# First loads in one queue, more tile pairs turned by DMA, one copy on another engine, and the last gate gradient later

## The chip, the cores and the metric

The kernel runs on one core of a Trainium2 chip. The core has a matrix engine (TensorE, called PE in the profile), a vector engine (DVE), a scalar engine (ACT), a general engine (GpSimd, called POOL) and a sync engine (SP) that mainly issues DMA transfers. Sixteen DMA engines move the data. The engines run their own instruction streams, each in order, and wait for one another through semaphores.

The metric is the device time of one execution, in microseconds (us). The median of three runs of the kernel before is 925.81 us (924.9 to 925.99).

## The reference

The program computes a forward pass and seven gradients. S is 2048 tokens, D is 512, F is 1376; there are 32 heads of 16 and an attention window of 256 tokens. In short:

```
g   = sigmoid((x * gate_w).sum(-1))            # one gate for each token
a   = sliding_window_attention(x @ wqkv) @ wo  # 32 heads, window 256
b   = (relu(x @ W_gate) * (x @ W_up)) @ W_down
out = g * a + (1 - g) * b
gradients of out for x, wqkv, wo, W_gate, W_up, W_down, gate_w, given grad_out
```

Both branches are called with x, which is the input `A_x`.

## The kernel before

The kernel has three stages that follow one another on TensorE.

**Stage 1 (up to about 250 us): the feed-forward branch, forward and backward.** The tokens are cut into four groups of 512 (`tg`, `NTG` = 4) and the 1376 hidden columns into eleven chunks of 128 (`fc`, `FC` = 11). That makes 44 steps. A step n does the gate product (`gate`, line 345), the up product (`up`, line 350), and, some steps later, the hidden gradient (`dh`, at step n + 2), the turning of the results by DMA (`turn_h`, `turn_dgu`) and the weight gradients (`weights`, at step n + 6). In the first four steps the loop at line 428 also turns x (`turn_x`), computes the gates of the tokens (`gate_col`), scales grad_out (`db_rows`) and turns that (`turn_db`).

The schedule of a stage is written by hand (`tc.manual_schedule()`): each engine's instructions stand in the order in which the Python code issues them.

Ahead of the first step come the loads. SP's queue issues x of the first group in two halves (line 234), then x of the second group, grad_out of the first, a piece of W_down, and so on (lines 254 to 263), all in the order of the code. ACT's queue issues `gate_w` and the first 128 columns of W_gate and of W_up (lines 237 to 239). Meanwhile TensorE runs eight warm-up products on zeros (`WARM`, lines 206 and 244). Then it turns `gate_w` into a column (`turn_gw`, line 417, called at 425), turns x of the first group (`turn_x(0)`), and starts the first gate product.

**Stage 2 (about 252 to 722 us): attention, forward and backward.** The 32 heads form four groups of eight (`c`), the queries sixteen blocks of 128 (`j`), and each block of queries meets up to three blocks of keys (`kb`). Heads go in two halves of four (`half`). One unit is one (c, j, kb, half); there are 360. Its role is `d` for the block on the diagonal, `m` for the middle one and `f` for the far one. For a unit TensorE makes the scores (`front`, line 656, tile `ST`), ACT takes the exponential (668), GpSimd masks roles d and f (670, 673), TensorE makes the gradient's score product (`front_dp`, 682, tile `dPT`), DVE multiplies (`gradp`, 687), and three units later (`LAG`) TensorE sums rows (`rowsum`, 696 and 698, tile `BA`).

The probabilities and their gradients are also needed turned, as the stationary operand of the products in `cd_piece` (lines 518 and 521, tile `CD`). `flip` (line 707) turns them in one of two ways. With `u.dma` a DMA transpose does it (line 715), for both halves at once where `u.pair` holds, and for one half otherwise. Without `u.dma`, TensorE makes eight transposes (line 725), and ACT and DVE in turn copy the result out of PSUM. The choice is made at lines 643 and 644: role d always goes as a pair; role m as a pair in odd rows of the first three head groups; in the other rows of role m only half 0 goes by DMA; role f never. Pairs of role m live in tile `PPm` (two buffers), single halves in `PPs` (one buffer).

The projections of the next four blocks (`project_parts`, line 118) and the weight gradient of the previous head group (`grad_parts`, line 598) are fed in between units, whenever a running `credit` (line 915) is high enough; a unit with TensorE transposes lowers that credit by 0.44. The projection of Q is scaled and copied out of PSUM by DVE (line 140) into `zT`, is spread by SP into the tile that the score products read (line 499), and is turned by DMA (line 171).

**Stage 3 (about 730 to 925 us): the outputs.** Sixteen tiles of 128 tokens (`t`, line 994). A tile makes the two branches' outputs (lines 1001 and 1005), the gradient of x (tile `dxps`: 22 products at line 1032, then 12 at line 1047), and the gate gradient: DVE and GpSimd compute `dz` from the outputs, `add_dgw` (line 1035) multiplies x with it, one tile late, through `pending_dgw`. Only the last tile has no later tile, so it adds its own share at once (lines 1042 to 1044), and in the middle of its last twelve products the gradient is turned into a row and stored (lines 1050 to 1055). The last instruction of the program is the store of the last `dx_sb` (line 1059).

Of the kernel before, what the change touches and what calls it, by code (L numbers as in the profile page):

```python
# [22 lines left out]
def kernel(  # L23
# [20 lines left out]
    nc = tc.nc  # L44
# [67 lines left out]
    if True:  # L112
        HH = HG // 2
        proj = {}
        groups = [(c, tg) for c in range(DC) for tg in range(NTG)]
        PENG = ("dvs", "dvs")

        def project_parts(c, tg):
            t4 = {}
            proj[(c, tg)] = t4  # L120
            pj = pjA if (c * NTG + tg) % 3 == 0 else pjs["b"]

            def mm(nm, which, eng):
                ps, tag, bufs, _, _ = pools["now"]
                pp = ps.tile([P, TGW], F32, tag=tag, bufs=bufs, name="pp")
                for cd in range(DC):
                    if which < 3:
                        nc.tensor.matmul(pp[:], lhsT=w_p[c][:, cd, which * P:(which + 1) * P], rhs=x_T[tg][:, cd, :],  # L128
                                         start=(cd == 0), stop=(cd == DC - 1))
                    else:  # L130
                        nc.tensor.matmul(pp[:], lhsT=w_p[c][:, cd, 3 * P:4 * P], rhs=da_T[tg][:, cd, :],
                                         start=(cd == 0), stop=(cd == DC - 1))
                if nm in ("Q", "dO"):
                    if nm == "Q":
                        t4["z"] = pjA.tile([P, 2, TGW], BF, tag="zT", name="zT")
                    dst = t4["z"][:, ("Q", "dO").index(nm), :]
                else:
                    dst = pjA.tile([P, TGW], BF, tag="T", bufs=2, name=f"{nm}T")[:]
                if nm == "Q":
                    nc.vector.tensor_scalar(dst, pp[:], scale, None, op0=ALU.mult)  # L140
                else:
                    evac(dst, pp[:], eng)
                t4[nm] = dst
                if nm in ("Q", "dO"):
                    if c == 0 and tg == 0:
                        w = ("Q", "dO").index(nm)
                        for k in range(NP):
                            rows = slice(32 * k, 32 * k + 32)
                            evac(zt[0][rows, w, k, :, :], dst[rows, :].rearrange("p (k q) -> p k q", k=TPG),
                                 (("dve", "act")[w] if k % 2 else "dve"))  # L150
                else:
                    for k in range(2):
                        t4[f"{nm}{k}"] = pj.tile([P, TGW], BF, tag=f"{nm}{k}", name=f"{nm}{k}")
                        if PENG[k] == "act":
                            nc.scalar.mul(t4[f"{nm}{k}"][:], pp[:], par[:, k:k + 1])
                        elif PENG[k] == "dve":
                            nc.vector.tensor_scalar(t4[f"{nm}{k}"][:], pp[:], par[:, k:k + 1], None, op0=ALU.mult)
                        else:
                            nc.vector.tensor_scalar(t4[f"{nm}{k}"][:], dst[:], par[:, k:k + 1], None, op0=ALU.mult)

            def tr(a_nm, b_nm):
                _, _, _, ps, trt = pools["now"]
                pt = ps.tile([P, 2, TPG, P], BF, tag=trt, bufs=2, name="ptp")
                for a, nm in enumerate((a_nm, b_nm)):
                    for k in range(TPG):
                        nc.tensor.transpose(pt[:, a, k, :], t4[nm][:, k * P:(k + 1) * P], ident[:])
                return pt

            def tr_rows():
                rows = pjA.tile([P, 2, TPG, P], BF, tag="rows", bufs=2, name="rows")  # L170
                nc.sync.dma_start_transpose(out=rows[:].rearrange("p a t d -> p (a t) d"),
                                            in_=t4["z"][:].rearrange("p a s -> p (a s)"))
                t4["rows"] = rows

            def tr_kv():
                kv = pj.tile([P, TPG, HG, 34], BF, tag="KV1", name="KV1")
                nc.gpsimd.memset(kv[:, :, :, 0:1], -1.0)
                nc.gpsimd.memset(kv[:, :, :, Dh + 1:Dh + 2], 1.0)
                pt = tr("K", "V")
                v = lambda a: pt[:, a, :, :].rearrange("p k (h d) -> p k h d", h=HG)  # L180
                nc.vector.tensor_scalar(kv[:, :, :, 1:1 + Dh], v(0), scale, None, op0=ALU.mult)
                nc.vector.tensor_copy(kv[:, :, :, Dh + 2:2 * Dh + 2], v(1))
                t4["kv"] = kv

            return [lambda: mm("Q", 0, "dve"), lambda: mm("dO", 3, "dve"), tr_rows, lambda: mm("K", 1, "act"),
                    lambda: mm("V", 2, "act"), tr_kv]

    with ExitStack() as p1, tc.manual_schedule():
# [14 lines left out]
            return ap[tg * TGW:(tg + 1) * TGW, :].rearrange("(t p) d -> p t d", p=P)  # L203

        W0 = P
        WARM = 8
        Wg_v, Wu_v = (w.rearrange("(c p) f -> p c f", p=P) for w in (B_W_gate, B_W_up))
        go_in, da_in = {}, {}

# [23 lines left out]
        for i in range(2):  # L233
            nc.sync.dma_start(x_r[:, i * half:(i + 1) * half, :], rows_of(x_d, 0)[:, i * half:(i + 1) * half, :])
        gw_r = fp.tile([P, P], BF, tag="upm", name="gw_r")
        nc.vector.memset(gw_r[:], 0.0)
        nc.scalar.dma_start(gw_r[0:DC, :], gate_w.rearrange("(c p) -> c p", p=P))
        nc.scalar.dma_start(Wg_sb[:, :, 0:W0], Wg_v[:, :, 0:W0])
        nc.scalar.dma_start(Wu_sb[:, :, 0:W0], Wu_v[:, :, 0:W0])
        nc.vector.memset(tiny[:], 0.0)  # L240
        nc.scalar.activation(tiny[:], tiny[:], ACT.Sigmoid)
        make_identity(nc, ident[:])
        wps0 = ps1.tile([P, TGW], F32, tag="mm", bufs=3, name="warm_ps")
# [6 lines left out]
        def load_wgu(a, b):  # L250
            nc.sync.dma_start(Wg_sb[:, :, a:b], Wg_v[:, :, a:b])
            nc.sync.dma_start(Wu_sb[:, :, a:b], Wu_v[:, :, a:b])

        load_x(1)
        load_go(0)
        nc.sync.dma_start(wd0[:], B_W_down[0:P, :])
        load_x(2)
# [164 lines left out]
        DA0 = 2 * NTG  # L422
        pools["now"] = (ps1, "tr", 2, ps1, "tr")
        first = []
        turn_gw()
        turn_x(0)
        stores = {}
        for n in range(N1 + 8):
            at = lambda lag: steps[n - lag] if 0 <= n - lag < N1 else None
            if at(0):  # L430
                gate(at(0))
                if n < NTG:
                    gate_col(n)
                if n == 2:
                    turn_wd0()
                if n + 1 < NTG:
                    turn_x(n + 1)
                up(at(0))
                if n < NTG:
                    db_rows(n)  # L440
                if at(0).tg == 0 and at(0).fc > 0:
                    turn_wd(at(0).fc)
# [43 lines left out]
    if True:  # L486
# [145 lines left out]
        for c in range(DC):  # L632
            for j in range(NT):
                kbs = [k for k in (j - 1, j, j - 2) if k >= 0]
                for half in range(2):
                    order = kbs if half or len(kbs) < 3 else [kbs[0], kbs[2], kbs[1]]
                    for ki, kb in enumerate(order):
                        u = Unit()
                        u.c, u.j, u.kb, u.half = c, j, kb, half
                        u.first = ki == 0 and half == 0  # L640
                        u.last = ki == len(kbs) - 1 and half == 1
                        u.role = ("d", "m", "f")[j - kb]
                        u.pair = u.role == "d" or (u.role == "m" and j % 2 == 1 and c < DC - 1)
                        u.dma = u.pair or (u.role == "m" and half == 0 and (c < DC - 1 or j < 10))
                        units.append(u)
        NU = len(units)
# [318 lines left out]
    with ExitStack() as p56:  # L965
        x_r5 = x_r

        with ExitStack() as p6:
# [20 lines left out]
            for g in range(NG):  # L989
# [3 lines left out]
                for tl in range(GT):  # L993
# [45 lines left out]

                    if pending_dgw is not None:  # L1040
                        add_dgw(*pending_dgw)
                    if t == NT - 1:
                        add_dgw(t, dz_bf)
                        nc.scalar.copy(dgw_sb[:, 0:DC], dgw_ps[:])
                    pending_dgw = (t, dz_bf)
                    for cc in range(C3):
                        nc.tensor.matmul(dxps[:], lhsT=T_g[:, 4 * (cc % DC) + cc // DC, lsl], rhs=W6[("wqkv", cc)],  # L1047
                                         start=(i == 0), stop=(i == nmm - 1))
                        i += 1
                        if t == NT - 1 and cc == C3 // 2:  # L1050
                            row_ps = ps6r.tile([P, P], BF, tag="aps", bufs=1, name="row_ps")
                            nc.tensor.transpose(row_ps[:], dgw_sb[:], ident[:])
                            row_sb = t6.tile([P, P], BF, tag="row_sb", bufs=1, name="row_sb")
                            nc.scalar.copy(row_sb[0:DC, :], row_ps[0:DC, :])
                            nc.sync.dma_start(out_7.rearrange("(c p) -> c p", p=P), row_sb[0:DC, :])
# [34 lines left out]
```

## Time and profile before

| | |
|---|---|
| median of three runs | 925.81 us (924.9 to 925.99) |
| the profiled execution: time | 926.6 us |
| the profiled execution: span, first to last instruction | 924.9 us |
| busy: TensorE / weight loads / DVE / ACT / GpSimd | 910.0 / 577.1 / 489.9 / 447.2 / 486.4 us |
| mean granted TensorE clock | 0.996 |
| data moved by DMA | 166.49 MB, mean 180 GB/s |

The profile page cuts the span into forty slices of 23 us. These three of its rows give tenths of the slice in which TensorE was busy, tenths of the full clock that TensorE was granted, and tenths that the DMA engines were busy:

```profile
PE   7999999999999999999999999999999999999998
...
PEclk8999999999999999999999999999999999999999
DMA  9889889999699999978999889999999799777841
```

Only the first and last slices show a TensorE that is not fully occupied, and only the first a lower clock. The DMA engines are busy through nearly all of the program. A busy TensorE is not a TensorE at its peak, since products are pipelined and each line counts from its start to its modelled end.

The costliest waits of the other engines are not repeated here: an engine that waits for TensorE, while TensorE is busy, costs nothing by that.

### The profile page before, as it was taken

How to read it: one execution, taken by the hardware profiler on the slowest of the kernel's cores; microseconds unless marked ns; L12 is line 12 of the kernel's file. 1: busy time of each engine (PE TensorE's matmuls, PEld its weight loads, DVE VectorE, ACT ScalarE, POOL GpSimd, SP SyncE). 2: the span in 40 equal slices, each digit the busy share in tenths (PEclk: the TensorE clock that was granted, in tenths of full speed). 3: DMA queues.
4: the chain of work that ended last, by engine and by line, in shares of the span. 5: the costliest groups of instructions: out<-in, count | busy, mean ns of one | idle time of the engine just before them, and what ended most of it. 6: DMA issues, size and time to landing. Idle time of an engine off the chain costs nothing.

```text
span 924.9 us, 26637 instructions
## 1 busy us (share of the span) xinstructions
PE 910.0 (98%) x10878; PEld 577.1 (62%) x10878; DVE 489.9 (53%) x910; ACT 447.2 (48%) x784; POOL 486.4 (53%) x937
## 2 busy tenths in 40 slices
PE   7999999999999999999999999999999999999998
PEld 5566565656657767667776677767777644444443
DVE  3433334435377777657776577766677222222223
ACT  4522322222268777667776677766688301111111
POOL 2644444545276767766777567776677311111111
PEclk8999999999999999999999999999999999999999
DMA  9889889999699999978999889999999799777841
GB/s 300 178 177 197 191 191 200 218 222 204 164 163 164 167 173 170 185 150 163 178 147 183 168 153 172 179 179 180 169 159 206 178 255 238 186 186 185 182 91 47
DMA packets 484635, 166.49 MB, mean 180 GB/s; under 512 B 408800, under 2 KB 483392, under 8 KB 484512
## 3 DMA queue, kind: packets, MB, share of 16 engines
q1 hardware_dynamic: 462808, 142.63, 82.9%
q10 hardware_dynamic: 20072, 17.57, 7.2%
q0 software_dynamic: 1632, 4.59, 1.4%
q8 instruction: 85, 1.39, 0.6%
q14 instruction: 38, 0.31, 0.1%
HBM read 32.28 MB, written 36.24 MB: 74 GB/s over the span
## 4 chain that ended last, share of the span: by engine, by line
PE 81%; POOL 5%; DMA 4%; ACT 3%; issue 3%; DVE 2%; SPq 1%; ACTq 0%; POOLq 0%; DVEq 0%
PE dxps L1032 8%; PE ST L656 7%; PE wps L391 7%; PE dPT L682 7%; PE pt L725 6%; PE dxps L1047 5%; PE wps L611 4%; PE gps L342 4%; PE bps L1001 4%; PE ups L342 4%; PE CD L518 4%; PE dhps L342 3%; PE dps L393 3%; PE BA L696 3%; PE pp L128 3%
## 5 line engine op out<-in xcount | busy, mean ns | idle before, releaser
L670 POOL TENSOR_SCALAR_AFFINE_SELECT PPd<-PPd 128x512 bf16<-128x512 bf16 x128 | 81.2, 634 | 113.8 <-ACT PPd L668 113.0
L687 DVE TENSOR_TENSOR Pd<-Pu,dPT 128x512 bf16<-128x512 bf16 x154 | 103.9, 678 | 67.8 <-POOL Pu L673 63.1
L656 PE MATMUL ST<-z,K 128*128 128x512 bf16 x360 | 135.9, 378 | 3.1 <-ACT PPd L668 0.9
L682 PE MATMUL dPT<-z,V 128*128 128x512 bf16 x360 | 136.0, 378 | 0.7 <-DVE Pd L687 0.2
L668 ACT ACTIVATE Pu<-ST 128x512 bf16<-128x512 f32 x154 | 92.6, 601 | 45.9 <-PE ST L656 45.2
L356 POOL TENSOR_TENSOR hT<-rg,upm 128x512 bf16<-128x512 bf16 x44 | 51.3, 1167 | 117.7 <-DVE upm L354 109.2
L391 PE MATMUL wps<-dgu_r,x_r 128*128 128x256 bf16 (+1 forms) x704 | 103.9, 270 | 0.2
L687 DVE TENSOR_TENSOR PPd<-PPd,dPT 128x512 bf16<-128x512 bf16 x128 | 87.2, 681 | 21.3 <-POOL PPd L670 20.0
L668 ACT ACTIVATE PPd<-ST 128x512 bf16<-128x512 f32 x128 | 77.3, 604 | 22.4 <-PE ST L656 20.2
L391 PEld LDWEIGHTS <-x_r 128*128 128x128 bf16 x704 | 68.3, 98 | 31.0 <-issue 0.7
L673 POOL TENSOR_SCALAR_AFFINE_SELECT Pu<-Pu 128x512 bf16<-128x512 bf16 x112 | 71.7, 640 | 21.2 <-ACT Pu L668 20.4
L1010 ACT COPY a_sb<-aps 128x512 f32<-128x512 f32 x16 | 9.4, 586 | 151.7 <-issue 137.7
L354 DVE SCALAR_TENSOR_TENSOR upm<-rg,ups 128x512 bf16<-128x512 bf16 x44 | 30.1, 684 | 81.4 <-PE ups L342 41.1
L348 ACT ACTIVATE rg<-gps 128x512 bf16<-128x512 f32 x44 | 26.3, 598 | 95.1 <-PE gps L342 54.2
L393 PE MATMUL dps<-db_r,h_r 128*128 128x512 bf16 x176 | 66.7, 379 | 0.0
L366 POOL TENSOR_TENSOR dgu<-dh_sb,rg 128x512 bf16<-128x512 bf16 x44 | 57.5, 1307 | 5.3 <-ACT dh_sb L362 5.3
L725 PE MATMUL pt<-ident,Pd 128*128 128x128 bf16 x616 | 59.5, 219 | 0.0
L725 PE MATMUL pt<-ident,Pu 128*128 128x128 bf16 x616 | 59.0, 217 | 0.0
L1016 POOL DMA_DIRECT2D out_dram<-o_sb x16 | 8.7, 541 | 88.5 <-DVE o_sb L1014 82.1
L72 ACT COPY p<-pt 128x1024 bf16<-128x1024 bf16 x51 | 52.4, 1028 | 1.2
L696 PE MATMUL BA<-KV,Pu 128*128 128x33 bf16 x616 | 51.0, 178 | 0.0
L611 PE MATMUL wps<-rows_st,x_r 128*128 128x384 bf16 x256 | 50.3, 325 | 0.0
(186 smaller groups left out, 2365.2 us busy)
## 6 DMA issues: line engine op xcount, KB each, us to landing
dqkvo_d<-rows_st SPq DMA_DIRECT2D x15, 512.0 KB, 4.0
hT_d<-hT ACTq DMA_DIRECT2D x44, 128.0 KB, 2.6
dgT_d<-dgu ACTq DMA_DIRECT2D x44, 128.0 KB, 2.9
duT_d<-dgu ACTq DMA_DIRECT2D x44, 128.0 KB, 3.0
duT_g<-duT_d SPq DMA_DIRECT2D x8, 640.0 KB, 5.7
gt<-hT_d SPq DMA_DIRECT2D x7, 640.0 KB, 5.5
dgT_g<-dgT_d SPq DMA_DIRECT2D x7, 640.0 KB, 5.7
z<-zT SPq DMA_DIRECT2D x60, 64.0 KB, 2.3
```

The lines of the kernel that those rows point to most:

```text
L342: nc.tensor.matmul(out[:], lhsT=w(c), rhs=x(c), start=(c == 0), stop=(c == DC - 1))
L391: nc.tensor.matmul(acc["w"][:, c, 0:2 * nw], lhsT=x_r[:, t, c * P:(c + 1) * P], rhs=k.dgu_r[:, :, i, s0:P], start=(go_ and c % 2 == 0), st ...
L393: nc.tensor.matmul(acc["d"][:], lhsT=k.h_r[:, i, :], rhs=db_r[:, t, :], start=go_, stop=no_)
L611: nc.tensor.matmul(wps[:], lhsT=x_r[:, t, part * P:(part + 1) * P], rhs=sts[c][:, t, 0:3, :], start=first and t == t0, stop=last and t == ...
L656: nc.tensor.matmul(ST[:], lhsT=KTt[:, ksl], rhs=z[:, 0, :, jl, :], start=True, stop=True)
L668: nc.scalar.activation(u.Pu[:], ST[:], ACT.Exp)
L670: nc.gpsimd.affine_select(out=u.Pu[:], in_=u.Pu[:], compare_op=ALU.is_ge, fill=0.0, base=0, pattern=[[0, HH], [1, P]], channel_multiplier=-1)
L682: nc.tensor.matmul(u.dPT[:], lhsT=VTt[:, ksl], rhs=z[:, 1, :, jl, :], start=True, stop=True)
L687: nc.vector.tensor_tensor(out=u.Pd[:], in0=u.Pu[:], in1=u.dPT[:], op=ALU.mult)
L696: nc.tensor.matmul(BA[:, h, 0:33], lhsT=u.Pu[:, hh, :], rhs=kv[:, u.kb % TPG, h, 1:34], start=(u.first and hh == 0), stop=True, skip_group ...
L725: nc.tensor.transpose(pt[:, a, hh, :], src[:, hh, :], ident[:])
L1032: nc.tensor.matmul(dxps[:], lhsT=src[:, fc, lsl], rhs=W6[(wt, fc)], start=(i == 0), stop=(i == nmm - 1))
```

## The change

- The three loads on ACT's queue move to SP's queue. The first columns of W_gate stand behind the two halves of x; `gate_w` and the first columns of W_up stand behind x of the second group.
- `turn_gw` moves from ahead of the first `turn_x` to behind the first gate product, and in step 0 `gate_col` moves behind the up product. One of eight warm-up products is left out.
- In `project_parts`, Q of the second group (`groups[1]`) is scaled by ACT instead of DVE.
- In head groups 1 and 2, role m of rows 4, 6 and 8 goes as pairs: half 1 is turned by DMA together with half 0, where TensorE turned it.
- In the last tile, the last `add_dgw` and its copy come after four of the last twelve products, and the row is turned after nine instead of seven.

```diff
-                if nm == "Q":
+                if nm == "Q" and (c, tg) == groups[1]:
+                    nc.scalar.mul(dst, pp[:], scale)
+                elif nm == "Q":
                     nc.vector.tensor_scalar(dst, pp[:], scale, None, op0=ALU.mult)
...
-        WARM = 8
+        WARM = 7
...
         gw_r = fp.tile([P, P], BF, tag="upm", name="gw_r")
+        nc.vector.memset(tiny[:], 0.0)
         nc.vector.memset(gw_r[:], 0.0)
-        nc.scalar.dma_start(gw_r[0:DC, :], gate_w.rearrange("(c p) -> c p", p=P))
-        nc.scalar.dma_start(Wg_sb[:, :, 0:W0], Wg_v[:, :, 0:W0])
-        nc.scalar.dma_start(Wu_sb[:, :, 0:W0], Wu_v[:, :, 0:W0])
-        nc.vector.memset(tiny[:], 0.0)
         nc.scalar.activation(tiny[:], tiny[:], ACT.Sigmoid)
...
+        nc.sync.dma_start(Wg_sb[:, :, 0:W0], Wg_v[:, :, 0:W0])
         load_x(1)
+        nc.sync.dma_start(gw_r[0:DC, :], gate_w.rearrange("(c p) -> c p", p=P))
+        nc.sync.dma_start(Wu_sb[:, :, 0:W0], Wu_v[:, :, 0:W0])
         load_go(0)
...
-        turn_gw()
         turn_x(0)
...
                 gate(at(0))
-                if n < NTG:
+                if n == 0:
+                    turn_gw()
+                elif n < NTG:
                     gate_col(n)
...
                 up(at(0))
+                if n == 0:
+                    gate_col(n)
...
-                        u.pair = u.role == "d" or (u.role == "m" and j % 2 == 1 and c < DC - 1)
+                        u.pair = u.role == "d" or (u.role == "m" and c < DC - 1 and (j % 2 == 1 or (c > 0 and j in (4, 6, 8))))
                         u.dma = u.pair or (u.role == "m" and half == 0 and (c < DC - 1 or j < 10))
...
-                    if t == NT - 1:
-                        add_dgw(t, dz_bf)
-                        nc.scalar.copy(dgw_sb[:, 0:DC], dgw_ps[:])
                     pending_dgw = (t, dz_bf)
                     for cc in range(C3):
...
-                        if t == NT - 1 and cc == C3 // 2:
+                        if t == NT - 1 and cc == C3 // 4:
+                            add_dgw(t, dz_bf)
+                            nc.scalar.copy(dgw_sb[:, 0:DC], dgw_ps[:])
+                        if t == NT - 1 and cc == C3 * 2 // 3:
                             row_ps = ps6r.tile([P, P], BF, tag="aps", bufs=1, name="row_ps")
```

## The prediction

> **What bounds the kernel now.** I read the busy shares first: TensorE is busy for 910.0 of 924.9 us, and no other engine passes 53%. Then I asked which waits TensorE has. They are few, and these are the two that the change touches (us in total, times, longest):
>
> ```profile
> PE gps L342 <- DMA Wg_sb<-in_B_W_gate_dram: 3.1, 1, 3.1
> ...
> PE dgw_ps L1037 <- DVE dz_bf L1026: 0.4, 1, 0.4
> ```
>
> So time can only come from TensorE's own work, from its first 15 us, or from its clock. The timeline of the start (start, us, engine, line, operation):
>
> ```profile
> 1.27 3.43 PE L245 MATMUL warm_ps<-warm 128*128 128x512 bf16 x8 [1.27 <-DVE warm L231]
> ...
> 4.59 1.06 PE L276 MATMUL ptx<-ident,x_r 128*128 128x128 bf16 x16
> ...
> 5.70 1.07 ACT L72 COPY x<-ptx 128x512 bf16<-128x512 bf16 x2 [1.22 <-DVE x L74]
> ...
> 8.71 1.89 PE L342 MATMUL gps<-x,Wg_sb 128*128 128x512 bf16 x4 [3.06 <-DMA Wg_sb<-in_B_W_gate_dram]
> ...
> 10.87 1.87 PE L276 MATMUL ptx<-ident,x_r 128*128 128x128 bf16 x16
> ...
> 12.53 1.91 PE L342 MATMUL ups<-x,Wu_sb 128*128 128x512 bf16 x4
> ...
> 14.23 1.24 PE L342 MATMUL gps<-x,Wg_sb 128*128 128x512 bf16 x4
> ```
>
> The operands of the first gate product were ready at 6.77, when ACT's copies end. Its weights came at 8.7. And the same sixteen transposes that took 1.06 us at 4.59 take 1.87 us at 10.87. The stretches say why (PE busy, PEld, DVE, ACT, POOL, granted clock, DMA share, GB/s):
>
> ```profile
> 5.70:8.70 3.00, 0.00 (x0) 0.00 (x0) 0.41 (x1) 1.07 (x2) 0.00 (x0) 0.85 1.08 313
> 8.70:11.00 2.30, 2.29 (x22) 1.20 (x23) 0.00 (x0) 0.36 (x1) 0.00 (x0) 0.50 1.09 353
> 11.00:14.60 3.60, 3.60 (x22) 2.28 (x20) 0.98 (x3) 2.13 (x5) 0.00 (x0) 0.50 1.10 350
> ```
>
> During the idle 3 us the granted clock falls, and it stays at half until 14.6. The wait thus costs itself and half speed on what follows. Why the weights are late, from the transfers (KB, us from issue to landing):
>
> ```profile
> x_r<-in_A_x_dram SPq DMA_DIRECT2D x3, 512.0 KB, 8.1
> ...
> p2m<-PPm SPq DMA_TRANSPOSE x30, 5.2
> ...
> p2m<-PPs SPq DMA_TRANSPOSE x24, 3.7
> ...
> Wg_sb<-in_B_W_gate_dram ACTq DMA_DIRECT2D x1, 128.0 KB, 6.8
> ```
>
> 128 KB take 6.8 us on ACT's queue beside SP's 512 KB loads; the two 256 KB halves of x, ahead of everything in SP's queue, take 3.0 us.
>
> **The start.** Queue order becomes x (512 KB), Wg (128), x1 (512), gate_w (1), Wu (128), go0 (512). At the 313 to 353 GB/s of the rows above 128 KB are 0.4 us; twice that for their short rows gives 0.8. The second x half was issued at 1.28 and landed 3.1 us later, at 4.4; Wg behind it lands near 5.2, x1 1.5 us later near 6.7, gate_w with it, Wu near 7.5, go0 near 9. SP issues three more transfers ahead of go0, at 0.43 to 0.58 us each by ACT's rows: 1.6 us, hidden, since these lines stand behind 1 MB of traffic anyway.
>
> One warm-up matmul less (0.43 us) and the gate_w transpose gone from the front let the x transposes start near 4.3, so the copies end near 6.4. The gate product's first two matmuls can run before that, the last two after: issued by 6.85. Then, at the full-speed spacing of the rows after 16 us: gate_w transpose 0.1, sixteen transposes 0.89, up product 0.86, gate column 0.54. The second gate product starts near 9.3 instead of 14.23: 4.9 us. I take off 0.5 for gate_w or x1 landing a little after 6.85, and use 4.4. If the clock halves all the same, at 7.82 as in this trace, some 3.1 us of that are lost again (6.8 us at half speed, of which the sixteen small gate-column matmuls do not slow): 1.5 is the lower end, 4.9 the upper.
>
> What is late next: x2 (needed near 10.9, lands near 10.9 by the same spacing), then nothing that I can see. The large weight remainders still drain near 24 us, and the turned hidden tiles queue behind them; the first weight-gradient product needs those at 36.8 now, near 32 then. From 24 us to 225 TensorE has no idle row worth 0.1 us, so a microsecond won at the start is a microsecond at the end.
>
> A sentence apart: the Trainium skill ("DMA: Bandwidth & Descriptors", Issuing engines are not separate DMA queues) says that issuing from several engines only saves sequencer time, since all share the same sixteen DMA engines. Read as "the queue does not matter", it would set this part at zero and the whole at 922.8; the 6.8 us against 3.0 agree that the engines are shared, and show that sharing is what delays the first weights.
>
> **Six pairs by DMA.** Units with role m in rows 4, 6, 8 of head groups 1 and 2 now go as pairs. Half 0 went by DMA already; half 1 had eight TensorE transposes and one copy. 48 transposes leave TensorE. One flip in the timeline:
>
> ```profile
> 400.77 0.38 PE L725 MATMUL pt<-ident,Pu 128*128 128x128 bf16 x4
> ...
> 400.99 0.39 PE L725 MATMUL pt<-ident,Pd 128*128 128x128 bf16 x4
> ...
> 401.22 0.38 PE L682 MATMUL dPT<-z,V 128*128 128x512 bf16 x1
> ```
>
> 0.45 us from the first transpose to the next product; 6 x 0.45 = 2.7. TensorE's idle share in 400 to 600 us is 0.74 of 200, so nearly all is real: 2.6 (0 to 2.9). Six copies of 0.68 (DVE) or 1.03 us (ACT) go too; both engines are busy for some 70%, so worth nothing. The DMA side pays 5.2 - 3.7 = 1.5 us for each pair. What hides it is the lead of the products that read the pair: they run when the next row is through, six units of some 1.3 us (360 units between 251.9 and 718.5 us) and the lag of three: 11 us or more after the issue, against a landing of 5.2 (6.7 at most). The longer SP instruction (2.37 us against 1.41, by the rows of the flip line) holds back the spreads of the next Q by 1.0; the first of them is issued at 257.6 and read by the fifth row, eighteen units or 23 us into the stage. The strips where it lands have room (same columns as above):
>
> ```profile
> 410.00:420.00 10.00, 10.00 (x179) 7.61 (x178) 6.78 (x12) 6.74 (x13) 5.91 (x15) 1.00 0.56 129
> ...
> 530.00:540.00 10.00, 10.00 (x193) 7.70 (x192) 6.34 (x13) 7.46 (x13) 6.68 (x17) 1.00 0.55 128
> ```
>
> The planner also gets 0.44 more credit for each of the six, so projections are fed a unit or so earlier: the same work, no price.
>
> **Q of the second group on ScalarE.** It ran on DVE from 253.35 to 254.04, and a score product waited 0.32 us for it. On ACT it takes 0.60 us from 253.35 on, in front of the second exponential, which then ends near 254.55 instead of 254.17; its mask on GpSimd and its gradient product follow 0.4 later. The score product goes 0.1 earlier. Bounds -0.3 to +0.4; I use 0, since ACT has 1.05 us idle before its next exponential but one.
>
> **The last gate gradient.**
>
> ```profile
> 918.38 0.24 PE L1037 MATMUL dgw_ps<-dz_bf,x_r 128*128 128x1 bf16 x4 [0.39 <-DVE dz_bf L1026]
> 918.38 0.14 PEld L1037 LDWEIGHTS <-x_r 128*128 128x128 bf16 x3 [0.46 <-issue]
> ...
> 922.10 0.35 SPq L1059 DMA_DIRECT2D out_dram<-dx_sb  x1
> ```
>
> Four products of 0.22 us now stand ahead of it, so the 0.39 us are filled: 0.4 (0.3 to 0.5). The row's transpose goes two products later, but its store is issued some 1.1 us before the dx store in SP's queue still: nothing.
>
> **Sum.** 4.4 + 2.6 + 0 + 0.4 = 7.4. The profiled execution had a span of 924.9 and a time of 926.6, which becomes 917.5 and 919.2. It lay 0.8 over the median of the runs, 925.81; that becomes 918.4.
>
> **Rivals.**
> Half clock (0.20). The clock falls at the start in spite of the shorter gap. For it: TensorE still pauses near 5.5 to 6.2 for the copies, and a fixed grid of time could catch that; two stretches at 0.50 followed work that was 74% busy. Against: the fall in this trace needed 3 us with no matmul at all. Start 1.5, whole 4.5: 921.3. The Trainium skill ("TensorE: Matmul & The Clock Gate", Part 1: The HAM clock gate) describes a free-running window of about 3.4 us that must be busy to release the clock and idle to lower it, so it would differ from run to run; the 3 us gap here agrees with it.
> The flips are not worth their time (0.07): TensorE fills the gap with other waits, as at 700 or 260 us. Sum 4.8: 921.0.
> One queue gains nothing (0.06): Wg's short rows go slowly and x1 and go0, issued 1.6 us later, are waited for instead. Start 0, whole 3.0: 922.8.
> Slower (0.08): the pairs fill the DMA queue in rows 3 to 9, where every row would now carry two full pairs. Added work 6 x 1.5 = 9.0 us; once the backlog has eaten the 6 us between landing and first use, TensorE waits for the added time instead of saving its transposes: 9.0 against 4.4 + 0.4, so 930.0. It decides from the point where more than 4.8 of the 9.0 stand on the path; short of it the time is near today's. Against it: the DMA share is 0.55 to 0.56 in two of the strips, and no wait of TensorE for a turned pair shows. For it: shares of 1.14 and 1.25 in 400 to 410 and 500 to 510.
>
> **Chances.** The forecast holds with 0.59. The first three rivals are faster too: 0.92. The last splits into slower, 0.05, and same, 0.03 (0.2%, 1.9 us, is about what a measurement of this kernel can tell). Range: from the best of each part, 4.9 + 2.9 + 0.3 + 0.5 = 8.6, to 917.2 and rounded down to 917.0, up to 922.0, which takes in the half clock and the lost flips and leaves out the last two rivals.
>
> **What would show it.** Right: no wait of the first gate product for Wg, a granted clock at 1.0 before 14 us, the second gate product near 9.5 to 10, p2m turned from PPm 36 times and from PPs 18 times (30 and 24 now), 48 fewer transposes at the flip line with no more idle time of TensorE than now in 370 to 560 us, and no 0.39 before the last gate-gradient product. Wrong: 0.50 in the clock after 7 us; waits for p2m or z in rows 4 to 9; a new wait for x or Wu in the first 15 us.

## The result and the profile after

The changed kernel takes 929.15 us (median of 6 runs, 928.31 to 929.77) where the kernel before takes 925.36 (6 runs, 923.14 to 926.2): ratio 1.0044, 95% interval 1.0031 to 1.0057. The forecast was 918.4. The profiled execution took 928.77, with a span of 927.1.

The waits of TensorE in the changed kernel (us in total, times, longest; in the views below, the line of before stands first). The wait for Wg went from 3.1 to 0.7 and the one for dz_bf is gone. But the score products' wait for the exponentials that write PPs, which stood at 0.6 (one time) before, is now the longest, and a wait of the same kind for PPm is new:

```profile
PE ST L656 <- ACT PPs L668: 0.6, 1, 0.6
```
```profile
PE ST L661 <- ACT PPs L673: 6.5, 3, 3.5
PE ST L661 <- ACT PPm L673: 1.3, 1, 1.3
...
PE gps L344 <- DMA Wg_sb<-in_B_W_gate_dram: 0.7, 1, 0.7
...
PE ptg L421 <- DMA gw_r<-in_gate_w_dram: 0.6, 1, 0.6
```

The start answers to the timeline shown of before. The second gate product begins at 10.19 instead of 14.23, and the sixteen transposes at 8.02 take 1.07 where they took 1.87:

```profile
1.27 3.17 PE L244 MATMUL warm_ps<-warm 128*128 128x512 bf16 x7 [1.27 <-DVE tiny L238]
4.23 1.27 PE L278 MATMUL ptx<-ident,x_r 128*128 128x128 bf16 x16
6.16 1.11 PE L344 MATMUL gps<-x,Wg_sb 128*128 128x512 bf16 x4 [0.66 <-DMA Wg_sb<-in_B_W_gate_dram]
7.83 0.23 PE L421 MATMUL ptg<-ident,gw_r 128*128 128x128 bf16 x1 [0.57 <-DMA gw_r<-in_gate_w_dram]
8.02 1.07 PE L278 MATMUL ptx<-ident,x_r 128*128 128x128 bf16 x16
...
10.19 1.02 PE L344 MATMUL gps<-x,Wg_sb 128*128 128x512 bf16 x4
```

Its stretches (busy us of PE, PEld, DVE, ACT and GpSimd, then granted clock, DMA share, GB/s) show a full clock although TensorE pauses:

```profile
4.00:9.00 5.00, 3.78 (x40) 2.48 (x38) 1.33 (x4) 1.67 (x3) 0.00 (x0) 1.00 1.00 293
9.00:16.00 7.00, 6.41 (x86) 4.26 (x84) 4.72 (x9) 5.61 (x10) 3.59 (x3) 1.00 1.12 345
```

To see where the time went I took the start of the first score product (ST) of each row in both traces. The difference, after minus before, in us (such differences are called the ledger below; each rests on one execution of either kernel):

| head group, row | 0,0 | 1,4 | 1,12 | 1,13 | 2,4 | 2,12 | 2,13 | 3,15 |
|---|---|---|---|---|---|---|---|---|
| after - before | -3.50 | -3.61 | -5.63 | +0.27 | -0.24 | -1.51 | +2.18 | +2.28 |

The pairs gain 2.0 between rows 4 and 12 of head group 1 and 1.3 in head group 2, as flips taken from TensorE should. Then row 12 costs 5.9 and 3.7 more than before. On ScalarE's timeline of the changed kernel, in row 12 of head group 1:

```profile
443.87 0.60 ACT L673 ACTIVATE Pu<-ST 128x512 bf16<-128x512 f32 x1 [0.30 <-PE ST L661]
448.99 0.60 ACT L673 ACTIVATE PPs<-ST 128x512 bf16<-128x512 f32 x1 [4.52 <-DMA p2m<-PPs]
```

The exponential of row 12 writes PPs, of which there is one buffer. It still holds row 10's half unit until that has been turned. SP's queue says when that turn went out, at 444.96, after row 9's two pairs and a weight load (a transposing transfer of weights from DRAM). In the kernel before, row 10's turn went out at 444.11, 5.8 ahead of row 12's first score product, and nothing waited for it. The first line is of before:

```profile
444.11 1.45 SPq L715 DMA_TRANSPOSE p2m<-PPs  x1
```
```profile
437.46 3.56 SPq L720 DMA_TRANSPOSE p2m<-PPm  x1
441.14 1.98 SPq L720 DMA_TRANSPOSE p2d<-PPd  x1
443.17 1.69 SPq L561 DMA_TRANSPOSE p<-in_A_wqkv_dram  x1
444.96 1.79 SPq L720 DMA_TRANSPOSE p2m<-PPs  x1
```

Behind the exponential stand the score products, since the four PSUM buffers that they share with the gradient's score products are full. In stretches of the changed kernel:

```profile
440.00:445.00 5.00, 5.00 (x108) 3.81 (x105) 4.41 (x8) 3.96 (x8) 3.48 (x9) 1.00 1.08 192
445.00:450.00 5.00, 1.51 (x14) 0.61 (x13) 1.67 (x3) 0.60 (x1) 2.39 (x6) 0.84 1.24 181
450.00:455.00 5.00, 5.00 (x49) 2.94 (x48) 1.01 (x3) 2.96 (x5) 1.64 (x3) 0.50 1.14 211
455.00:460.00 5.00, 5.00 (x92) 3.61 (x91) 3.94 (x7) 3.39 (x5) 3.03 (x8) 0.98 0.64 129
```

TensorE stands 3.5 us, and then the clock is at half: of the 5.9, some 3.5 are the wait, and by my estimate most of the rest is work at half speed.

### The profile page after: what moved, and what is told of

The parts are those of the page before. It is cut to its first block, busy times and chain, and to the rows that moved or that the text cites. A ratio compares the mean times of both kernels' runs of the same rounds, so it can differ in the third digit from the quotient of the medians.

```text
span 927.1 us, 26527 instructions
## 1 busy us (share of the span) xinstructions
PE 907.7 (98%) x10829; PEld 574.0 (62%) x10829; DVE 488.1 (53%) x906; ACT 446.9 (48%) x782; POOL 487.7 (53%) x937
## 4 chain that ended last, share of the span: by engine, by line
PE 86%; DMA 4%; POOL 4%; ACT 3%; issue 1%; DVE 1%; SPq 0%; ACTq 0%; POOLq 0%; DVEq 0%
PE dxps L1037 8%; PE wps L393 8%; PE ST L661 8%; PE dPT L687 7%; PE pt L730 6%; PE dxps L1049 5%; PE wps L616 4%; PE dps L395 4%; PE CD L523 4%; PE bps L1006 4%; PE BA L701 4%; PE pp L128 4%; PE ups L344 4%; PE dhps L344 4%; PE gps L344 3%; PE CD L526 2%
## 5 line engine op out<-in xcount | busy, mean ns | idle before, releaser
L692 DVE TENSOR_TENSOR Pd<-Pu,dPT 128x512 bf16<-128x512 bf16 x148 | 99.9, 679 | 67.7 <-POOL Pu L678 53.8
L673 ACT ACTIVATE Pu<-ST 128x512 bf16<-128x512 f32 x148 | 88.8, 600 | 37.7 <-PE ST L661 36.8
L128 PE MATMUL pp<-x,p 128*128 128x512 bf16 x192 | 49.0, 378 | 0.5 <-ACT PPd L673 0.2
```

Of the source, the lines that this page charges most:

```text
L673: nc.scalar.activation(u.Pu[:], ST[:], ACT.Exp)
L692: nc.vector.tensor_tensor(out=u.Pd[:], in0=u.Pu[:], in1=u.dPT[:], op=ALU.mult)
```

## The experiments

Each ratio is to the kernel before on the same chip, with its 95% interval. "Changed" and "before" in a heading say which kernel the edit starts from.

**Changed, without the six pairs.**
```diff
-u.pair = ... c < DC - 1 and (j % 2 == 1 or (c > 0 and j in (4, 6, 8))))
+u.pair = u.role == "d" or (u.role == "m" and j % 2 == 1 and c < DC - 1)
```


> The changed kernel with the six pairs taken back (rows 4, 6, 8 of head groups 1 and 2 as before), the other three parts kept. Theory A (the six pairs alone lose the time, at rows 12 and 13 of head groups 1 and 2; start and end are worth 3.5 and about 0.3): 921 to 922.5, that is 3.3 to 4.2 below the kernel before, and no wait of ScalarE above 2 us for a p2m turned from PPs. Rival B (the loss comes from the shifted phase of the stages after the earlier start, or from Q on ScalarE, and not from the pairs): 926 or more, with the two losses at row 13 still there.


922.95 against 925.16, 0.9973 (0.996 to 0.9986). From head group 1 on, no exponential waits for PPs on a DMA; one wait of 1.5 us is left, at row 12 of head group 0, where before has one of 1.6. The mechanism of theory A holds, though the time lies 0.45 above its range: the other three parts bring 2.2 by the medians, 2.5 by the ratio, and not 3.3 or more.

**Before, with the six pairs alone.** The same line, the other way.


> The kernel before with the six pairs alone. Theory A: the ledger of the changed kernel has gains of 2.0 and 1.3 in the even rows and losses of 5.9 and 3.7 at row 13, together +6.3; so some 931 to 932.5, with waits of ScalarE for p2m<-PPs of 3 to 5 us in rows 12 of head groups 1 and 2. Rival B: the pairs gain their 2.6 here and the time is near 923. If only the phase decides whether the backlog is caught, something in between.


932.33 against 925.16, 1.008 (1.0063 to 1.0097), with the waits at row 12 (ScalarE 7.7 us for p2m from PPs, two times). The pairs alone cost 7.

**Changed, a second buffer for the half units.**
```diff
-nh, tag, bufs = 1, "PPs", 1
+nh, tag, bufs = 1, "PPs", 2
-tag="P2f", bufs=4
+tag="P2f", bufs=3
```


> The changed kernel, where the half units that go by DMA alone have two buffers instead of one (the room comes from one of the four buffers of the tiles that TensorE has turned). Theory A1 (the single buffer is the place where the late turn of row 10 stops the exponential of row 12; the queue itself has room to recover): the losses at row 13 go, and the time is 918.5 to 920.5. Rival A2 (the transposing transfers are saturated and a buffer more only moves the wait, to PPm or to the products that read the turned pair): 923 or more, and the wait turns up under another tile. If the fourth buffer was needed, new waits for P2f in all head groups would show.


923.62, 0.9988 (0.9977 to 1.0). Between the theories, and the ledger shows both at work: nothing is lost at row 12 of either head group, and the lead over before grows to 6.6 at the start of head group 3; then 4.3 of it go in rows 0 to 2 there, under another tile, PPd (these ledgers are against the first profile of before).

**Changed, row 10 turned by TensorE.**
```diff
-(c < DC - 1 or j < 10))
+(c < DC - 1 or j < 10) and not (c in (1, 2) and j == 10))
```


> The changed kernel, where row 10 of head groups 1 and 2 sends no half unit by DMA: TensorE turns both halves (two flips more at 0.45 us each). Theory A1 (it is row 10's late turn that row 12 waits for): nothing is left to wait for, the losses of 5.9 and 3.7 go, the price is 0.9: 919.5 to 921. Rival A2 (saturated transfers): the backlog of rows 4 to 9 meets the next tile in its way, PPm of row 11 or 13, and more than half of the loss stays: 924 or more.


924.09, 0.9994 (0.9984 to 1.0003). The losses at row 12 go, as A1 says. The time is A2's, 924 or more: the price is a little higher than I put it (0.5 and 0.6 between rows 10 and 12), and 1.5 is lost at the start of head group 3, with a wait of ScalarE for p2d of 2.9.

**Changed, weight loads one group of rows later** (plan keys 7 and 11 become 8 and 12).


> The changed kernel with the four transposing loads of wqkv that run in rows 9 to 13 of head groups 1 and 2 (two each) moved one group of rows later. If these loads make the turn of row 10 late (theory B1: each is an instruction of about 1.25 to 2.4 us in SP's queue ahead of it), the waits of 4.5 and 3.5 us at row 12 mostly go: 921 to 924. If the pairs alone fill the queue (theory B2) the loss stays within 1.5 of today's: 927 to 930.


922.89 against 924.38, 0.9986 (0.9975 to 0.9997). B1: row 12 loses 1.1 in place of 5.9 in head group 1 and nothing in head group 2. But 2.7 are lost at the start of head group 3, where the loads now stand.

**Two buffers, weight loads barred from rows 0 to 3 of head group 3.**


> The second buffer for the half units as in the earlier run, and none of the weight loads that transpose is issued in rows 0 to 3 of head group 3 (they follow from row 4 on, every second unit instead of every third). If these loads make the p2d turns late that cost that run 4.3 us there, this one keeps its lead of 6.6 through head group 3: 918 to 920.5. If the lead is lost there anyway, or later at rows 4 to 15 where the loads are now closer together: 922 or more.


923.91, 0.9995 (0.9982 to 1.0007): the lead was lost again. The edit missed its mark. Four loads were still queued in rows 13 to 15 of head group 2, and SP reached them late, two of them in head group 3. ScalarE and SP of this run:

```profile
601.67 0.60 ACT L673 ACTIVATE PPd<-ST 128x512 bf16<-128x512 f32 x1 [3.85 <-DMA p2d<-PPd]
```
```profile
593.77 1.32 SPq L561 DMA_TRANSPOSE d<-in_B_W_gate_dram  x1
595.19 2.62 SPq L720 DMA_TRANSPOSE p2d<-PPd  x1
597.86 1.41 SPq L561 DMA_TRANSPOSE d<-in_B_W_gate_dram  x1
```

**Changed, the spreads issued by GpSimd** (`nc.gpsimd.dma_start` in spread).


> The changed kernel with the spreads of Q and dO (four 64 KB transfers for each group of rows) issued by GpSimd instead of SP; the same transfers otherwise. If SP's own instruction time is the limit (theory C1: SP gets back 2.5 to 3.4 us of each group of 31 us) the backlog shrinks and the time is 922 to 926. If the transfers themselves are (theory C2: the transposing turns have their rate, and SP's instructions only last long because the ring is full), it stays at 928 to 931; and if GpSimd's masks are held up by the issue, above 931.


936.42, 1.0132 (1.0115 to 1.0149): the third case. Once in each group of rows GpSimd waits for zT and then issues, with its masks queued behind (four spreads in one row):

```profile
335.72 2.17 POOL L504 DMA_DIRECT2D z<-zT  x4 [1.37 <-DVE zT L74]
```

It doesn't tell whether SP's instructions or the transfers are the limit; that stays open.

**Changed, four pairs** (`j in (4, 6)`).


> The changed kernel with pairs in rows 4 and 6 only of head groups 1 and 2, row 8 as before: four more pairs in place of six. If the backlog grows with each pair and is paid back only by row 10 (theory A), the last pair before row 10 counts most, and the waits at row 12 fall from 4.5 and 3.5 to 2 or less each: 920 to 924. If any backlog over rows 4 to 6 costs the same (the loss does not depend on the number): 927 or more.


923.2, 0.9997 (0.9983 to 1.0011). Row 12 loses 1.2 and 0.6, as theory A has it: without row 8's pair, the last before row 10, most of the loss goes.

**No weight load that transposes between row 8 of head group 2 and row 3 of head group 3**, with two buffers, with one, and without the pairs.
```diff
-if late and (u is None or n % 3 == 1):
+if late and (u is None or (gi < 10 and n % 3 == 1) or (u.c == DC - 1 and u.j > 3 and n % 2 == 1)):
```


> The changed kernel with two buffers for the half units, and with no weight load that transposes between row 8 of head group 2 and row 3 of head group 3 (they follow from row 4 of head group 3 on). In the run before, four of these loads still stood in SP's queue in rows 13 to 15 of head group 2, so that the strip where the lead of 6 was lost had not been relieved. Theory D (the queue of transposing transfers is full from row 9 of a head group to row 3 of the next, and what the six pairs put in must be taken out there): head group 3 row 3 keeps 6 or more of the lead, 916.5 to 919. Rival (the wait for p2d there has another cause: three buffers for four diagonal pairs in rows 14, 15, 0 and 1): 922 or more, with the same wait.


919.14 against 924.89, 0.9933 (0.9918 to 0.9948).


> The changed kernel with its single buffer, and the weight loads moved as in the run beside it; the two loads of wqkv in head group 1 stay. Theory D: head group 1 loses its 5.9 as before, head group 2 and the start of head group 3 lose nothing: 922 to 924.5. If the single buffer alone makes the loss: the loss of 3.7 in head group 2 stays, and the time is 926 or more.


923.39, 0.9987 (0.9972 to 1.0002).


> The changed kernel without the six pairs, and with the weight loads moved as in the runs beside it. It tells what the room in the queue is worth by itself: without the pairs nothing waits for a turned tile in head groups 1 to 3, so theory D gives the time of the first run without pairs, 921 to 923, and the run with pairs and two buffers stands some 2.5 to 4 below it. If moving the loads helps by itself (fewer disturbances of other kinds), this one is faster than 921 too and the pairs are worth less.


922.54, 0.9971 (0.9962 to 0.9981). The second and third lie in theory D's ranges. The first lies 0.14 above its own: from row 11 of head group 3 on 1.6 are lost, and the third, which has no pairs, loses 1.4 there too. The profile of the second does not bear theory D out in full. It is the fastest of twelve executions (919.52); head group 2 loses 0.3, as forecast, but head group 1, where the code is that of the changed kernel, loses 2.7 and not 5.9. So the loss at row 12 differs by some 3 us from one execution to another. With room in the queue and a second buffer, the six pairs are worth 922.54 - 919.14 = 3.4; with neither they cost 7. The stretch at the start of head group 3, first with a second buffer only, then in the spaced version below:

```profile
595.00:615.00 20.00, 17.25 (x276) 11.70 (x273) 11.94 (x25) 11.85 (x23) 12.46 (x31) 0.91 1.02 195
```
```profile
595.00:615.00 20.00, 20.00 (x343) 14.15 (x342) 15.03 (x30) 14.28 (x27) 15.35 (x38) 1.00 1.00 165
```

**Before, with the start alone.**


> The kernel before with the start alone: the queue order, the warm-up of seven, the gate_w transpose behind the first gate product. The prediction gave it 4.4; the profiles of the changed kernel and its variants show the second to fourth gate product 3.2 to 3.7 earlier. If the ledger holds to the end: 921 to 922.3, ratio 0.996 to 0.9975. If part of it is lost again before the attention stage (one profile without pairs lost 1.2 between the gate products and the first score product): 922.5 to 923.5.


922.62 against 924.2, 0.9981 (0.997 to 0.9991), the second case: the start is worth 1.6 (0.8 to 2.8).

**Before, again.**


> The kernel before, unchanged, for a second profile, since all ledgers stand on one execution that lay 0.8 above the median of its runs. If the wait of 1.5 for p2d at the start of head group 3 belongs to the kernel, it is here again and the span is near 924; if it belongs to that execution, it is gone and the span is near 923, which takes 1.4 from every gain that was read against the first profile behind that point.


924.25, span 922.5, and no wait for p2d: it belonged to the first execution. Against this profile the changed kernel's lead at the first score product is 2.85, not 3.50, and rows 0 to 2 of head group 3 take 15.9, not 17.3.

**Before, with six turns more**, of a piece of x into a tile that nobody reads (P2f has three buffers for it).
```diff
+if u.role == "m" and u.half == 1 and u.c in (1, 2) and u.j in (4, 6, 8):
+    nc.sync.dma_start_transpose(out=<a spare tile>, in_=x_r[:, 0:2, :] as [P, 1024])
```


> The kernel before, which does all its own work, and beside it six turned tiles of 128x1024 more in SP's queue in rows 4, 6, 8 of head groups 1 and 2, read by nobody (one of the four buffers of the tiles that TensorE has turned makes room). Nothing is taken from TensorE, so what it loses is the price of the transfers alone. Theory D (a full queue, with the single buffer as the place where it bites): waits of ScalarE for p2m<-PPs at row 12 and 3 to 7 us lost: 928 to 932. If the pairs cost by something else (the pair's buffers, a later landing, the planner's other order), it stays within 1.5 of the kernel before.


925.27, 1.0011 (1.0 to 1.0021). Theory D as I had put it falls: the transfers alone cost about 1 us (0 to 1.9), and row 12 takes no longer than before. Row 10's turn goes out at 444.95, and the exponential of row 12 comes at 449.32 (SP, then ScalarE):

```profile
443.55 1.29 SPq L556 DMA_TRANSPOSE p<-in_A_wqkv_dram  x1
444.95 1.25 SPq L718 DMA_TRANSPOSE p2m<-PPs  x1
```
```profile
449.32 0.60 ACT L668 ACTIVATE PPs<-ST 128x512 bf16<-128x512 f32 x1
```

**Two buffers, weight loads after row 3 of head group 3, spaced** (`n % (2 if u.j < 10 else 3)`).


> The version with two buffers and all weight turns after row 3 of head group 3, which lost 1.6 at rows 11 and 12 of head group 3 to a wait for p2d while the loads stood closer than before. Here they go back to every third unit from row 10 on. If these loads make that wait: 917 to 918.5, and no wait for p2d there. If not: 919 to 920.


918.56 against 924.2, 0.9938 (0.9921 to 0.9954). The 1.6 at rows 11 and 12 are not lost here; the medians of the two versions lie too close to tell more.

**Changed, the halves of the six units turned apart.**
```diff
+solo = u.pair and u.role == "m" and u.j % 2 == 0
...
-hs = slice(0, 2) if u.pair else slice(u.half, u.half + 1)
+hs = slice(0, 2) if u.pair and not solo else slice(u.half, u.half + 1)
...
```


> The changed kernel, where each half of the six units is turned by a transfer of its own as soon as it is ready, 12 small turns in place of six large ones; buffers, weight loads and TensorE's work as in the changed kernel. Theory E (the six turns at no cost to TensorE lost nothing, 1.0011, so the bytes alone are not it; a pair is turned only when its later half is done, so SP's queue stands still in the middle of rows 6 and 8 and is behind by row 10): the first half goes into that gap again, row 10's turn is issued near 445 less the start instead of 449 less the start, and the losses of 5.9 and 3.7 fall to 1 or less: 918.5 to 921.5. Theory D (the bytes of the queue, with TensorE faster in front of it): twelve small turns are at least as long as six large ones (1.25 each by the shortest rows, 1.8 for a large one), so 927 to 931.


927.41 against 924.25, 1.003 (1.0017 to 1.0043). Row 12 loses 4.1 and 2.5 where it lost 5.9 and 3.7, and 1.9 are lost at the start of head group 3: theory E takes back a third of the loss at row 12, its forecast fails, and the time is in theory D's range.


> The fastest version so far (two buffers, weight loads after row 3 of head group 3) with the halves turned apart. Theory E: nothing was left to wait for there in head groups 1 and 2, so within 1 of 918.5. Theory D: the longer SP time costs here too, 920 or more.


917.52, 0.9927 (0.9914 to 0.9941): the fastest here, not told apart from 918.56.

**Before, the second halves replaced by a turn of x.**


> The kernel before, where TensorE no longer turns the second half of the six units, and a transfer of the same size turns a piece of x in its place (the second halves of these six units thus enter dK, dQ and dV wrongly). Bytes, number of turns and their order are those of the run with six turns more, which lost nothing; the source is always ready, so nothing waits for a later half; only TensorE is faster, by 2.0 and 1.3. Theory F (row 12 needs row 10's turn issued some 3.7 ahead; it had 6.7 and 5.3, six turns more left 3.8 and 4.7, and what TensorE gains in rows 4 to 10 comes off the rest): slack 1.8 and 3.4 or less, so head group 1 loses 2 to 3.5 at row 12, head group 2 up to 1: together 922.5 to 925. Theory E (only the wait for the later half makes the queue late): nothing lost, 3.3 gained, 920 to 921.5. If the bytes were the whole price, as with the pairs alone: 931 or more.


924.82 against 923.95, 1.0007 (0.9995 to 1.0018), as theory F says in the sum; row 12 loses 1.0 and 0.8, less than F said for head group 1. Against the second profile of before another 1.9 goes at the start of head group 3 (1.3 in the run with six turns more). So the pairs' bytes and TensorE's saving, without a wait for a later half, come to nothing together, where the pairs themselves cost 7.

## Why the prediction was wrong

**The step that failed** is that of the six pairs: "What hides it is the lead of the products that read the pair", 11 us against a landing of 5.2, and "The strips where it lands have room". The term stood in the sum as a gain of 2.6; alone the pairs measure a loss of 7. The readers were never late: no wait for p2m stands among TensorE's. The deadline was another, the next writer of the source buffer. PPs is one buffer, used by rows 10 and 12, and nothing in the working asked when it comes free. The signs of being wrong were looked for in rows 4 to 9; the wait came at row 12.

The trace of before held a warning. In row 12 of head group 0 the turn of row 10 went out 3.7 us ahead, ScalarE waited for PPs, the row took 8.5 where it takes 8.0 in the second profile (4.2 ahead there), and the chain of work that ended last ran through that turn (ScalarE's wait, then the chain's line: start, us):

```profile
ACT PPs L668 <- DMA p2m<-PPs: 1.6, 1, 1.6
```
```profile
326.71 5.38 DMA p2m<-PPs
```

The prediction's "no wait of TensorE for a turned pair shows" was true of pairs, but TensorE had waited 0.6 for a turned half. The measure of what followed is the time from the issue of row 10's turn to row 12's first score product (slack), and by how much row 12 then exceeds its undisturbed 7.7 in head group 1 and 8.0 in head group 2:

| kernel | slack, group 1 | row 12 longer by | slack, group 2 | row 12 longer by |
|---|---|---|---|---|
| before, first profile | 5.8 | 0 | 5.4 | 0 |
| before, second profile | 6.7 | 0 | 5.3 | 0 |
| changed, no pairs | 6.9 | 0 | 5.6 | 0 |
| before, six turns more | 3.8 | 0 | 4.8 | 0 |
| before, turns of x for second halves | 3.2 | 1.0 | 3.0 | 0.8 |
| changed, four pairs | 2.8 | 1.2 | 3.4 | 0.6 |
| changed, weight loads later | 2.7 | 1.1 | 3.6 | 0 |
| changed, no loads from row 8 of head group 2 | 0.3 | 2.7 | 3.6 | 0.3 |
| changed, halves apart | 1.0 | 4.1 | 0.1 | 2.5 |
| before, pairs alone | -0.3 | 5.0 | 0.8 | 3.5 |
| changed | -0.7 | 5.9 | 0.8 | 3.7 |
| changed, two buffers | -0.8 | 0.3 | -0.5 | 0 |

Below some 3.5 to 3.8 of slack the row pays, in every kernel of the table with one buffer; with two it hardly does (0.3 and 0). (The row of the changed kernel shows why: the turn goes out at 444.96, the buffer is free by 448.99, 4.0 later.) By these single executions three steps ate the 6.7 and 5.3; two executions of before differ by 0.9, and two of the code of the changed kernel by 1.0 in slack, so the small ones are within the scatter. The added transfers took 2.9 and 0.5 (six turns more: 3.8 and 4.8 are left). A faster TensorE took 0.6 and 1.8 more (turns of x: 3.2 and 3.0 are left): it comes to row 12 earlier by 1.8 and 1.1, and the queue does not follow in full, or not at all. The pairs as they are took another 3.5 and 2.2; in them a turn of both halves goes out only when the later half is done. This last is the largest in time: 1.0080 against 1.0007, some 7 us, at the same bytes and the same work taken from TensorE. What makes it up was not separated. With the halves turned apart no larger turn is left, and row 12 still lost 4.1 and 2.5, so the size of the turn is not the main part. The pairs also write to PPm instead of PPs, but no exponential waited for PPm in these two head groups. That leaves the turn of the second half, behind which SP's queue stands until its source is done; this is argued, not shown.

The strips that I quoted, 410 to 420 and 530 to 540, do have room. The one behind the first has not: the DMA share is 1.24 in the second of these lines of before:

```profile
415.00:435.00 20.00, 20.00 (x353) 14.19 (x350) 13.90 (x27) 15.07 (x29) 12.91 (x30) 1.00 0.86 172
435.00:455.00 20.00, 19.86 (x377) 14.53 (x374) 15.79 (x30) 14.60 (x27) 15.88 (x38) 1.00 1.24 166
```

A backlog made in rows 4 to 8 is paid in rows 9 to 13, where odd rows' pairs and two weight loads already fill the queue.

**The slower rival** gave 930.0 and had the queue right and the price wrong: TensorE does not wait for the added 9.0 us of transfers, which alone cost 1, but for one buffer, and the idle time then costs the clock. That its number lies near the 929.15 measured is luck.

**The pairs' gain** was under-sized: 2.6 predicted, 2.0 + 1.3 = 3.3 in the ledger before row 12, 3.4 between the versions with room.

**The start**: the mechanism is right (the first gate product at 6.2 in place of 8.7; the clock record, which begins at 4.66, shows no half before 448.40), the term of 4.4 is mis-sized. The first columns of W_gate, put near 5.2, landed near 6.1 (issued at 1.83, 4.3 to landing). The second gate product came 4.0 earlier, not 4.9, with 0.57 for gate_w, as allowed for; the third lost 0.5 more to waits of 0.27 and 0.32 ahead of the x transposes. By itself the start measures 1.6 (0.8 to 2.8). Its own profile ran 2.5 below the second profile of before; it was 3.0 ahead at the first score product and lost 0.6 at the start of head group 3. Of those 2.5, 0.9 belong to the execution, which lay that far below the median of its runs (921.73 against 922.62). The rival of the half clock did not come; for its "work that was 74% busy" I find no stretch in the trace of before, where 1.24 of the 3.41 us ahead of the fall were busy. The rival that one queue gains nothing, with the Trainium skill's "DMA: Bandwidth & Descriptors" (Issuing engines are not separate DMA queues), is refuted in that reading: the start with the order in the one queue was worth 1.6 as a whole (the order, the warm-up and the moved transpose were not measured apart), and the wait for Wg fell from 3.1 to 0.7. What the section says of several issuers, that they only save the sequencer's time, fits the run where GpSimd took over the spreads: SP no longer spends 3.75 us on four of them (at 421.68 of the changed kernel), GpSimd spends 2.17 behind a wait of 1.37, and the kernel took 936.42.

**Q on ScalarE**, put at nothing, is nothing: from row 0 to row 3 of head group 0 it takes 13.80 in both profiles of before, 13.81 after.

**The last gate gradient**, put at 0.4: from the first dx product to the last it takes 180.9 and 181.4 before, 180.4 in the versions without pairs. In the changed kernel it is 181.1, with a wait of 0.6 for duT_g that eats it. The products sit without a wait, and the row's transpose behind them:

```profile
921.45 0.24 PE L1042 MATMUL dgw_ps<-dz_bf,x_r 128*128 128x1 bf16 x4
921.55 1.24 PE L1049 MATMUL dxps<-p,gt 128*128 128x512 bf16 x5
922.62 0.22 PE L1057 MATMUL row_ps<-ident,dgw_sb 128*128 128x128 bf16 x1
```

**The sum** that the runs support: start 1.6 to 2.5 with the two small parts, pairs 3.4 where the queue has room, 5.6 together (924.2 - 918.56); as changed, the pairs turn it into a loss of 3.8.

## What to carry to other kernels

Work given to a queue has two deadlines: its reader, and the next writer of the buffer it reads from; count the buffers of the source before calling a transfer hidden, and take the queue's share over the rows that follow, not in the strip where the work lands. What speeds up an engine in front of a full queue shortens the slack of all that stands in the queue, so a saving and its cover must be worked out together. Move other transfers out of the way first, or add the buffer: here both were needed, one for each place where the backlog came out.

## What the runs showed of the hardware

The same transposing instruction of SP has no one duration: a turn of a half unit from PPs shows 1.25 and 2.76 us, a pair from PPm 1.64 and 3.72. A long one is not simply the sign of a busy strip: the 1.25 at 444.95 in the run with six turns more follows 5 us with a DMA share of 1.12. The runs do not show what an instruction spends the rest on, so SP's busy time is no measure of the transfers' work.

TensorE's wait of 3.5 us at row 12 of head group 1 halved the clock for 6.83 us by the trace's clock record, and its wait of 2.6 in head group 2 for 3.41. The Trainium skill ("TensorE: Matmul & The Clock Gate", Part 1: The HAM clock gate) describes a free-running window of about 3.4 us; both lengths are whole numbers of it, and there the trace agrees. That an idle window is needed does not fit as simply, and here the measurement decides: 2.6 us without work were enough, and in the run with the halves apart a wait of 2.6 was followed by these stretches:

```profile
445.00:450.00 5.00, 2.35 (x32) 1.26 (x30) 2.37 (x4) 0.79 (x2) 2.69 (x7) 0.92 0.93 176
450.00:455.00 5.00, 5.00 (x70) 3.37 (x69) 2.02 (x5) 3.55 (x7) 1.64 (x3) 0.74 1.12 209
```

The PE column of the first counts 2.35 busy of 5, the clock of the second is 0.74. So a wait shorter than the window can cost the clock too. Of the 3.41 us that end with the two falls in the changed kernel (444.98 to 448.40 and 567.86 to 571.28) the PE column counts 1.17 and 1.00 busy, and ahead of the fall at the start of before (4.41 to 7.82) 1.24, so the prediction's "the 3 us gap here agrees with it" holds only loosely. After 2.10 busy, from 608.82, the clock stayed up. Nor does a wait of this length always cost it: in the run with one buffer and no loads from row 8 of head group 2, with 2.51 busy of the 5 us from 445, the granted clock stayed at 1.00, and row 12 lost 2.7 instead of 5.9.
